# Two groups loaded two tokens to a partition, w spread by its DMA, and a new order of all steps

## The chip, the cores and the metric

The kernel runs on one core of a Trainium2 chip. The metric is device time in microseconds. The kernel before takes 174.13 us (median of three runs, 174.08 to 174.55).

A core has five engines that run side by side, each with an instruction queue of its own, worked off in order: TensorE (PE; PEld is its weight load), VectorE (DVE), ScalarE (ACT), GpSimd (POOL) and SyncE (SP), which here issues DMAs. An engine that waits for a semaphore holds up all that stands behind it in its queue.

## The reference

```python
def _attn_ref(r, k, v, w, u):            # B, H, S, D = 4, 8, 768, 48
    state = zeros((B, H, D, D))
    for t in range(S):
        cur = einsum('bhd,bhe->bhde', u * k_t, v_t)
        y[:, :, t] = einsum('bhd,bhde->bhe', r_t, state + cur)
        state = w * state + einsum('bhd,bhe->bhde', k_t, v_t)

def _moe_ref(x, w_in, w_out):            # 3072 tokens, 384, 2048
    h = x @ w_in
    g = where(h >= 1, h, where(h <= -1, 0, (h + 1) ** 2 / 4))
    return g @ w_out
```

The result of the first, token by token with its eight heads side by side, is the x of the second.

## The kernel before

The 768 tokens of a sequence are cut into six chunks of 128. A *unit* is one chunk of one batch, a *group* two batches of one chunk; there are 12 groups and 24 units, unit 2g + j being half j of group g. In a chunk the recurrence becomes matmuls: r is scaled by a rising power of w (`Rs`), k by a falling one (`Ks`), both are turned so that the head's dimension lies on partitions (into `TT`, or by a DMA into `RT`, `KT`), `A` is their product over all pairs of tokens, masked into `AT`; `Y` is `AT` times v, plus r times the state before the chunk; `Sp` is k times v, the chunk's addition to the state. The u term is the sum over d of r·k·u (`KU`, `RKU`, `us` into `diag`) times v (`B`), added to Y when y is written. y is turned (`X` and `xc`, or one DMA, `xcg`) into `xT`. Then the second part: `m` (12 matmuls) makes a quarter of h, `r`, `s`, `g` make the activation, `M` (4 matmuls) multiplies by a quarter of w_out, `og` copies the sum out of PSUM and `stg` stores it.

The order of all work is written out by hand in the string ORDER, which a loop reads from left to right. A word names a step, `do_` plus the letters: `Ks1.0=G/2` would be step Ks of group 1, half 0, on POOL (V is DVE, A is ACT), with PSUM bank 2. `m2.3` is quarter 3 of group 2, `M2.13` half 1, quarter 3. Each word puts instructions at the end of its engine's queue, so the string fixes the order in each queue and nothing else; semaphores do the rest. Loads (`LR`, `LK`, `LV`) go to SP's queue, as do the DMA transposes and the stores, while the weights (`WI`, `WO`) are issued on POOL. `Z` steps are idle matmuls on zeros that fill TensorE's gaps.

In groups 0 and 1 (JOINT = 2) the work goes unit by unit, with A, Y, Sp and X in eight PSUM banks b0 to b3 and pairs p0, p1; then b0 to b3 are closed (`first.close()`) and become the pairs p2, p3. The first `m` with /2 or /3 is `m1.1`, so it waits until every step in a bank is done. For the tables of powers, w is loaded as one row, its logarithm is spread over the partitions with a matmul (`bw`, L207), and ACT takes Exp with the token's number as the scale (`Wdn`, `Wup`; `dn_t`, `up_t` are copies that live in PSUM).

In the load below a packet holds one token of one head, 48 f32 numbers, 192 bytes:

```python
nc.sync.dma_start(out=t[:, j0 * H : j1 * H, :], in_=source(x, g, j0, j1))   # L253
```

Of the kernel before, what the change touches and what calls it, by code (L numbers as in the profile page):

```python
# [610 lines left out]
```

## Time and profile before

| | us |
|---|---|
| median of the runs | 174.13 |
| span of the profiled execution | 172.6 |
| TensorE busy | 164.4 |
| DVE, ACT, POOL busy | 130.6, 129.9, 117.4 |
| first `m` starts | 19.21 |
| last matmul ends | 169.14 |
| w_row to Ln, first table on ACT | 2.87, 5.12 |

The span counts from the first instruction to the last; the profiled execution's own time is not given beside it, so its distance to the runs is read from their median. The tables of the profile that matter here are the busy shares, the chain of work that ended last, the table of stretches (busy time of each engine, granted clock), the timeline of instructions, the groups of instructions with their mean duration, and the DMA issues with the time to landing. In a row such as `out<-in` the names are the program's; in a timeline row the first number is the start, the second the duration, and the bracket at the end the idle time before it and what ended it.

### The profile page before, as it was taken

What the parts mean: (1) busy time and instruction counts of PE and PEld (TensorE: products, weight loads), DVE (VectorE), ACT (ScalarE), POOL (GpSimd) and SP (SyncE); (2) the same over time, 40 slices, a digit from 0 to 9 for tenths busy, and PEclk for the clock granted to TensorE, in tenths of its full rate; (3) what the DMA queues carried; (4) which work ended last, traced back from release to release, by engine and by line L of the source; (5) the groups of instructions that cost most, each with busy time, mean ns of one, the idle gap of its engine ahead of it and who ended that gap; (6) DMA issues with size and microseconds to landing.
All of it is one profiled execution on the core that took longest, in us unless ns stands there. A gap on an engine that the chain in (4) does not pass through costs nothing.

```text
span 172.6 us, 4051 instructions
## 1 busy us (share of the span) xinstructions
PE 164.4 (95%) x1674; PEld 132.9 (77%) x1674; DVE 130.6 (76%) x150; ACT 129.9 (75%) x150; POOL 117.4 (68%) x86
## 2 busy tenths in 40 slices
PE   7989968999999999989999999999999999999991
PEld 5769868966889777588787797696897787888871
DVE  4578698988687688859789779885889959873752
ACT  4355698991699899189979879689695896988940
POOL 3496744998689949999999998999568804300000
PEclk9999999999999999999999999999999999999999
DMA  6999999998996999999999997998999025140022
GB/s 114 194 184 179 199 187 180 228 210 174 206 191 99 206 184 168 194 199 145 196 312 210 182 220 163 223 182 155 297 170 267 4 52 145 37 104 0 8 91 91
DMA packets 103751, 28.26 MB, mean 164 GB/s; under 512 B 98866, under 2 KB 102836, under 8 KB 103732
## 3 DMA queue, kind: packets, MB, share of 16 engines
q1 hardware_dynamic: 101824, 24.75, 79.9%
q0 software_dynamic: 1760, 3.15, 9.8%
q8 instruction: 13, 0.21, 0.6%
q10 hardware_dynamic: 148, 0.10, 0.2%
q14 instruction: 6, 0.05, 0.1%
HBM read 20.45 MB, written 4.72 MB: 146 GB/s over the span
## 4 chain that ended last, share of the span: by engine, by line
PE 87%; ACT 4%; DMA 2%; DVE 2%; issue 1%; POOL 0%; ACTq 0%; DVEq 0%
PE hp L475 35%; PE op L512 34%; PE A L370 4%; PE Y L438 3%; DMA xT<-y 2%; PE Y L432 2%; PE Sp L405 2%; PE z L566 2%; ACT pt L486 1%; PE T L330 1%; ACT TT L112 1%; PE lwp L207 1%; PE wp L233 1%; PE TR L330 1%; PE TK L330 1%
## 5 line engine op out<-in xcount | busy, mean ns | idle before, releaser
L475 PE MATMUL hp<-xT,w_in 128*128 128x256 bf16 x576 | 69.1, 273 | 1.3 <-DMA xT<-y 0.8
L512 PE MATMUL op<-w_out,g 128*128 128x384 bf16 (+1 forms) x400 | 68.4, 320 | 0.0
L498 DVE SCALAR_TENSOR_TENSOR g<-sq,hp 128x1024 bf16<-128x1024 bf16 x48 | 57.9, 1215 | 13.2 <-ACT sq L495 13.2
L475 PEld LDWEIGHTS <-w_in 128*128 128x128 bf16 x576 | 61.9, 114 | 4.6 <-issue 1.6
L486 ACT ACTIVATE pt<-hp 128x1024 f32<-128x1024 f32 x46 | 46.9, 1021 | 13.7 <-PE hp L475 13.7
L512 PEld LDWEIGHTS <-g 128*128 128x128 bf16 x400 | 37.5, 98 | 20.4
L495 ACT ACTIVATE sq<-pt 128x1024 bf16<-128x1024 f32 x46 | 48.3, 1057 | 1.2
L379 DVE TENSOR_TENSOR AT<-A,umask 128x1024 bf16<-128x1024 f32 x20 | 23.7, 1220 | 5.2 <-PE A L370 5.2
L282 POOL TENSOR_TENSOR Ks<-Ki,Wdn 128x768 bf16<-128x768 f32 (+1 forms) x12 | 20.3, 1689 | 8.5 <-ACT Wdn L225 3.4
L313 POOL TENSOR_TENSOR V<-Vb,diag 128x768 f32<-128x768 bf16 (+1 forms) x14 | 18.1, 1291 | 9.8 <-DVE diag L304 4.4
L282 POOL TENSOR_TENSOR RKU<-Ri,KU 128x768 f32<-128x768 f32 (+1 forms) x13 | 21.2, 1630 | 1.1 <-DVE KU L282 0.7
L282 POOL TENSOR_TENSOR KU<-Ki,u_sb 128x768 f32<-128x768 f32 (+1 forms) x13 | 21.2, 1634 | 0.4 <-DMA Ki<-in_k_dram 0.4
L416 POOL TENSOR_TENSOR state<-Tm,wCm 128x768 f32<-128x768 f32 x8 | 14.6, 1824 | 9.8 <-DVE Tm L413 9.8
L282 POOL TENSOR_TENSOR Rs<-Ri,Wup 128x768 bf16<-128x768 f32 x10 | 18.2, 1820 | 0.3 <-DMA Ri<-in_r_dram 0.3
L112 ACT CAST Vb<-Vi 128x768 bf16<-128x768 f32 (+1 forms) x14 | 10.2, 733 | 5.4 <-DMA Vi<-in_v_dram 5.4
L450 DVE TENSOR_TENSOR y<-Y,V 128x768 bf16<-128x768 f32 x10 | 9.6, 956 | 5.9 <-PE Y L438 3.3
L304 DVE TENSOR_REDUCE diag<-RKU 128x16 f32<-128x768 f32 (+1 forms) x14 | 11.6, 831 | 1.5 <-POOL RKU L282 1.5
L112 ACT CAST state_bf<-state 128x768 bf16<-128x768 f32 (+1 forms) x12 | 8.5, 717 | 4.4 <-POOL state L416 4.4
L112 ACT COPY o<-op 128x768 f32<-128x768 f32 (+1 forms) x9 | 6.7, 748 | 6.0 <-PE op L512 5.9
L438 PE MATMUL Y<-Vb,AT 128*128 128x48 bf16 x192 | 10.4, 186 | 0.4 <-ACT Vb L112 0.4
L438 PEld LDWEIGHTS <-AT 128*128 128x128 bf16 x192 | 9.5, 98 | 0.7 <-issue 0.5
L413 DVE TENSOR_TENSOR Tm<-Sp,state 128x768 f32<-128x768 f32 x8 | 7.7, 956 | 3.1 <-PE Sp L405 3.1
(73 smaller groups left out, 123.3 us busy)
## 6 DMA issues: line engine op xcount, KB each, us to landing
out_dram<-o SPq DMA_DIRECT2D x11, 384.0 KB, 3.8
Ki<-in_k_dram SPq DMA_DIRECT2D x9, 384.0 KB, 6.2
Ri<-in_r_dram SPq DMA_DIRECT2D x9, 384.0 KB, 6.2
Vi<-in_v_dram SPq DMA_DIRECT2D x9, 384.0 KB, 5.4
Ki<-in_k_dram SPq DMA_DIRECT2D x6, 192.0 KB, 4.0
Ri<-in_r_dram SPq DMA_DIRECT2D x6, 192.0 KB, 4.7
Vi<-in_v_dram SPq DMA_DIRECT2D x6, 192.0 KB, 6.0
w_in<-in_moe_w_in_dram POOLq DMA_DIRECT2D x2, 384.0 KB, 7.5
```

The source lines that it names most:

```text
L112: nc.scalar.copy(out, in_) if e == "A" else engines[e].tensor_copy(out, in_)
L282: engines[e].tensor_mul(part(out)[:, :, :, :D], part(a), rep(b, j1 - j0) if len(b.shape) == 3 and b.shape[1] == H else part(b))
L304: nc.vector.tensor_reduce(d[:, hs], tiles["RKU", g][:, hs, :], AX.X, ALU.add)
L313: engines[e].tensor_mul(t[:, hs, :], tiles["V", g][:, hs, :], tiles["diag", g][:, hs].unsqueeze(2).to_broadcast([P, n, D]))
L379: nc.vector.tensor_mul(t.rearrange("p i n t -> p (i n) t"), tiles["A", n].rearrange("p i (n t) -> p (i n) t", t=P), umask.unsqueeze(1).to_ ...
L416: engines[e].tensor_mul(states[g % BP], tiles["Tm", g], flat(wCm).unsqueeze(1).to_broadcast([P, UNITS, DM]))
L438: nc.tensor.matmul(Y[:, h * D : (h + 1) * D], AT[:, i, p, :], V[:, j * H + h, :], start=(c == 0), stop=True, skip_group_check=True,)
L475: nc.tensor.matmul(hp[:, f, :], w_in_sb[wi][:, i, wo * FG * P + f : (wo + 1) * FG * P : FG], tiles["xT", g][:, :, i, :], start=(i == 0), s ...
L486: nc.scalar.activation(t, tiles["hp", g, q], AF.Relu, bias=0.5, scale=0.5)
L495: nc.scalar.activation(t, p, AF.Square)
L498: nc.vector.scalar_tensor_tensor(out=make("g", ("g", g, q), [P, FG, TOK], BF16), in0=tiles["sq", g, q], scalar=1.0, in1=tiles["hp", g, q], ...
L512: nc.tensor.matmul(tiles[key][:, i, : o1 - o0], tiles["g", g, q][:, f, j * P : (j + 1) * P], w_out_sb[wi][:, wo, f * DO + o0 : f * DO + o1 ...
```

## The change

**Loads.** For groups 0 and 1, R and K come in one DMA each (no `.0`, `.1`). Partition 2q + b holds tokens 2q and 2q + 1 of batch b, so a packet has two tokens, 384 bytes. V is loaded as before.

**Parity.** Step `Rs0.1` now means the odd tokens of both batches, not batch 1; the same for `Ks` (into a tile `Kt`), `KU`, `RKU`, `us` and the transposes `TR`, `TK`. The copies out of PSUM, `cR` and `cK`, sort the columns back into units and so read with a stride. As the scaled k no longer lies token by token, `BK` turns it back on TensorE and `kc` copies it to SBUF, four units each. The u sums are also by parity; `dP`, four f32 matmuls per group with a selection matrix, sorts them, and `dC` copies them out.

**w.** Its DMA spreads it over 128 partitions; Ln and all Exp work on that, with tables `U0`, `U1`, `D0`, `D1` for the parities and `Wup`, `Wdn` for the other groups. `bw` and `wq` go; the column w_col comes by two DMAs of single elements, issued on ACT.

**Order.** All of ORDER is new. In the count, `r` on DVE goes from 2 to 9 (ACT 46 to 39), one each of `Rs`, `KU`, `B` and two of `Ks` of the later groups go from POOL to DVE, `og` on DVE from 3 to 1. `M` steps of one PSUM sum need no longer begin with quarter 0. The last group's two half outputs get a pair each, and both half stores are issued on SP (`stA11.1` was on ACT).

DVE's queue in the head. Before, from the copy of u on: the scaled K and R by unit, then masks and sums.

```order
L112 COPY u_sb_115<-up_153 128x384
L282 TENSOR_TENSOR Ks_92<-Ki_151,dn_t_174 128x8x48 x2
L282 TENSOR_TENSOR Rs_88<-Ri_158,up_t_183 128x8x48
L282 TENSOR_TENSOR KU_195<-Ki_151,u_sb_115 128x384
L282 TENSOR_TENSOR Rs_88<-Ri_158,up_t_183 128x8x48
L304 TENSOR_REDUCE diag_228<-RKU_198 128x8
L384 TENSOR_TENSOR AT_238<-A1_213,umask_105 128x512
L282 TENSOR_TENSOR Rs_89<-Ri_171,Wup_113 128x8x48 x2
L384 TENSOR_TENSOR AT_261<-A0_244,umask_105 128x512
```

The same place now, behind the scaled `Rs0.1`, `Ks0.0`, `Ks0.1` and two `KU` (`pt` are the parity tables, `TT` the sorted transposes, `pairs` the u sums by parity, `dP` their sorted form in PSUM):

```order
L115 COPY TT_233<-TK_212 128x512
L115 COPY TT_233<-TR_190 128x512
L115 COPY TT_228<-TK_212 128x512
L323 TENSOR_TENSOR Ks_104<-Ki_195,pt_197 128x8x48
L348 TENSOR_REDUCE pairs_270<-RKU_220 128x8
L337 TENSOR_TENSOR RKU_220<-Ri_174,KU_218 128x384
L456 TENSOR_TENSOR AT_274<-A1_252,umask_117 128x512
L456 TENSOR_TENSOR AT_274<-A0_251,umask_117 128x512
L348 TENSOR_REDUCE pairs_270<-RKU_220 128x8
L456 TENSOR_TENSOR AT_302<-A0_286,umask_117 128x512
L456 TENSOR_TENSOR AT_302<-A1_287,umask_117 128x512
L115 COPY diag_321<-dP_304 128x16
```

Three copies that ACT had made stand on DVE ahead of the first mask, and the copy of the sorted sums stands between the masks and what writes y.

SP's queue, where the program begins. Before, unit by unit:

```order
L253 DMA Ki<-in_k_dram 128x8x48 x2
L253 DMA Ri<-in_r_dram 128x8x48
L253 DMA Ki<-in_k_dram 128x8x48
L253 DMA Ri<-in_r_dram 128x8x48
L253 DMA Vi<-in_v_dram 128x8x48
L253 DMA Ri<-in_r_dram 128x8x48 x2
L253 DMA Ki<-in_k_dram 128x8x48
L253 DMA Vi<-in_v_dram 128x8x48 x3
```

Now, with the joint loads as 8 runs of 96 numbers:

```order
L274 DMA Ri<-in_r_dram 128x8x96
L274 DMA Ki<-in_k_dram 128x8x96 x2
L281 DMA Vi<-in_v_dram 128x8x48 x2
L274 DMA Ri<-in_r_dram 128x8x96
L281 DMA Vi<-in_v_dram 128x8x48 x2
L281 DMA Ki<-in_k_dram 128x8x48 x2
```

R of group 0 now comes first, and two units of V stand ahead of R of group 1.

DVE's queue around the sum of y in group 7. Before:

```order
L379 TENSOR_TENSOR AT_1682<-A_1660,umask_105 128x1024
L379 TENSOR_TENSOR AT_1701<-A_1651,umask_105 128x1024
L498 SCALAR_TENSOR_TENSOR g_1703<-sq_1643,hp_1628 128x1024
L450 TENSOR_TENSOR y_1730<-Y_1705,V2_1649 128x768
L498 SCALAR_TENSOR_TENSOR g_1766<-sq_1738,hp_1684 128x1024
```

Now:

```order
L451 TENSOR_TENSOR AT_1712<-A_1690,umask_117 128x1024
L451 TENSOR_TENSOR AT_1722<-A_1699,umask_117 128x1024
L570 SCALAR_TENSOR_TENSOR g_1754<-sq_1679,hp_1660 128x1024
L485 TENSOR_TENSOR Tm_1760<-Sp_1737,state_147 128x768
L522 TENSOR_TENSOR y_1794<-Y_1764,V2_1789 128x768
L570 SCALAR_TENSOR_TENSOR g_1809<-sq_1792,hp_1724 128x1024
```

The state's sum `Tm` has moved ahead of the sum of y. On TensorE the words between the last Y of this group and its first `m` are, before and now:

```
Y14/0 Y15 ... m6.3/1 m6.2/2 ... Sp12/0 Sp13 ... M6.00/3 M6.10 M6.11 M6.01 ... m7.1/0
Y15/3 Y14 ... m6.2/2 ... m6.3/1 ... M6.01/3 M6.11 M6.00 ... m7.1/0
```

The core of the diff:

```diff
-    nc.scalar.dma_start(out=w_row, in_=w.rearrange("(o h) d -> o (h d)", o=1))
+    nc.scalar.dma_start(out=w_all, in_=w.rearrange("(o h) d -> o (h d)", o=1).to_broadcast([P, DM]))
...
+    nc.gpsimd.memset(w_col, 1.0)
+    for j in range(2):
+        nc.scalar.dma_start(out=w_col[j * HP : j * HP + D, :], in_=w.rearrange("(p j) d -> j d p", j=2)[j])
...
     def do_ln(e, b):
-        nc.scalar.activation(lnw[:, :, :D], w_row.rearrange("o (h d) -> o h d", h=H), AF.Ln)
+        nc.scalar.activation(w_all, w_all, AF.Ln)
...
+    def do_U(e, b, i):
+        nc.scalar.activation(paired("up2")[:, i], w_all, AF.Exp, scale=up2_col[i])
...
     def load(x, what, cls, g, j):
+        if g < JOINT and what != "V32":
+            t = make(cls, (what, g), [P, UNITS * H, D], F32)
+            b0 = g * UNITS
+            nc.sync.dma_start(
+                out=t.rearrange("p (h e) d -> p h (e d)", e=2),
+                in_=x[b0 : b0 + UNITS, :, :C, :].rearrange("b h (q e) d -> q (b h) (e d)", e=2),
+            )
+            return
...
+    def do_dP(e, b, g):
+        t = tiles["dP", g] = bank(b[0], [P, UNITS, H], F32, "dP")
+        for j in range(UNITS):
+            for i in range(2):
+                nc.tensor.matmul(t[:, j], sel[j][:, 1 + j - i : 1 + j - i + P], tiles["pairs", g][:, i * H : (i + 1) * H], start=(i == 0), stop=(i == 1))
...
+    def unpair(e, kind, n, i):
+        g, j = divmod(n, UNITS)
+        t = make("TT", ("TT", n), [P, 2 * NP, P], BF16)[:, i * NP : (i + 1) * NP]
+        copy(e, t.rearrange("x p (q e) -> x p q e", e=2), tiles[kind, g].rearrange("x e p (q b) -> x p q e b", b=2)[..., j])
...
+    def do_BK(e, b, n):
+        t = tiles["BK", n] = bank(b[0], [P, NP, P], BF16, "BK")
+        for p in range(NP):
+            nc.tensor.transpose(t[:, p, :], tiles["TT", n][:, NP + p, :], ident)
+
+    def do_kc(e, b, n):
+        g, j = divmod(n, UNITS)
+        copy(e, flat(scaled("Ks", g)[:, j * H : (j + 1) * H, :]), tiles["BK", n].rearrange("p n t -> p (n t)"))
```

217 lines of the change are left out of this document (126 added, 91 removed).

## The prediction

> **What bounds the kernel now.** First the page's busy shares, then the chain of work that ended last in order of time, then the table of stretches and the waits.
>
> ```profile
> PE 164.4 (95%) x1674; PEld 132.9 (77%) x1674; DVE 130.6 (76%) x150; ACT 129.9 (75%) x150; POOL 117.4 (68%) x86
> ...
> 19.28 1.45 PE hp L475 x12
> ...
> 27.27 6.73 PE hp L475 x60
> ...
> 57.76 1.31 PE hp L475 x12
> 59.07 0.65 PE op L512 x4
> ...
> 64.63 0.55 PE A L370 x16
> ...
> 69.80 4.27 DMA xT<-y
> 74.11 1.47 PE hp L475 x12
> ...
> 89.83 2.63 PE hp L475 x24
> ...
> 169.14 0.33 ACT o L112
> 169.49 0.36 DVE o L112
> ```
>
> ```profile
> 20.00:24.00 4.00, 3.03 (x42) 2.55 (x41) 3.70 (x8) 3.23 (x4) 1.24 (x2) 1.00 1.14 208
> 24.00:28.00 4.00, 3.12 (x41) 2.89 (x40) 3.68 (x7) 2.83 (x5) 1.92 (x3) 1.00 0.88 163
> ...
> 68.00:75.00 7.00, 6.16 (x73) 4.16 (x69) 6.01 (x6) 3.09 (x4) 6.92 (x5) 1.00 1.01 192
> ```
>
> The columns of the stretches are length, busy time of PE, PEld, DVE, ACT, POOL, then granted clock, DMA share, GB/s. TensorE is the bound: the chain lies on it from 19.28 us, the first `m0.0`, to 169.14, and its clock is full. One `m` step (12 matmuls) takes 1.31 us, one `M` (4) 0.65, one `AA` (16) 0.55. TensorE can win only what it idles, in three places. **The head** runs until `m1.1`, 27.27 + 1.31 = 28.58 us; by then both kernels have done the same: A, Y, X, Sp of four units and the four `m` of group 0. From 20 to 28 us TensorE idles 0.97 + 0.88 us, and before 19 us its gaps are filled with idle matmuls (`Z`). **The dense part**, 28.58 to 169.14, is 140.56 us and holds one gap of 0.84 us in 68 to 75. **The tail** is what follows 169.14. The span is 172.6 us and the runs' median 174.13, so 1.5 us lies around the span; I take that as unchanged.
>
> **The change, part by part.**
>
> *Tables.* In place of `bw`, four Exp and eight small matmuls there are a spread load of w, two element loads, Ln on all partitions and four Exp.
>
> ```profile
> 0.74 0.54 ACTq L127 DMA_DIRECT2D w_row<-in_w_dram  x1
> 1.31 0.23 ACTq L128 DMA_DIRECT2D u_row<-in_u_dram  x1
> 2.87 0.52 ACT L203 ACTIVATE lnw<-w_row 1x384 f32<-1x384 f32 x1
> 5.12 0.58 ACT L225 ACTIVATE Wdn<-lwp,dn_col 128x384 f32<-128x384 f32 x1 [1.73 <-PE lwp L207]
> 5.60 0.55 ACT L219 ACTIVATE dn_t<-lwp,dn_col 128x384 f32<-128x384 f32 x1
> Ki<-in_k_dram SPq DMA_DIRECT2D x1, 192.0 KB, 3.0
> 4.00:8.00 4.00, 4.00 (x15) 2.81 (x14) 1.60 (x4) 1.50 (x3) 1.81 (x2) 1.00 1.40 195
> ```
>
> The spread w is 192 KB. It lands between 2.87 (where Ln could start before) and 0.74 + 3.0 = 3.7 (the first load of K, equally large). Two more issues on ACT, 0.23 to 0.54 us each, stand ahead of Ln: it starts at 3.3 to 4.2, I take 3.7. Ln takes 0.55 and its reader waits for its end; each Exp follows the last by 0.48. So `U1` ends at 4.8, `U0` 5.3, `D0` 5.8, `D1` 6.2. Before, the first table ended at 5.70 and the second at 6.15.
>
> *Loads.* At 195 GB/s 192 KB pass in 1.0 us, so the first load spent 3.0 - 1.0 = 2.0 us on its way. A joint load of 384 KB costs 2.0 us at that rate. The other end comes from stores, whose packets are larger:
>
> ```profile
> out_dram<-o SPq DMA_DIRECT2D x1, 192.0 KB, 1.9
> out_dram<-o SPq DMA_DIRECT2D x1, 96.0 KB, 1.7
> ```
>
> 96 KB more cost 0.2 us, so 384 KB 0.8. 384 bytes are nearer to 192 than to a store's row: I take 1.4. With 0.3 for w, R of group 0 lands at 0.74 + 2.0 + 0.3 + 1.4 = 4.4, K at 5.9, K of group 1 at 7.3, two units of V by 9.2, R of group 1 at 10.6. By the Trainium skill, "DMA: Bandwidth & Descriptors", section Specifications, transfers under 512 B stay below line rate; no row here has 384-byte packets. By that the joint load stands at its dear end, which is rival B.
>
> *DVE sets the head.* From `Rs0.1` on it has 24 instructions in a row that lead to the last `xc` before `m0.0`.
>
> ```profile
> 11.34 1.02 DVE L282 TENSOR_TENSOR Rs<-Ri,Wup 128x384 bf16<-128x384 f32 x2
> L384 DVE TENSOR_TENSOR AT<-A,umask 128x512 bf16<-128x512 f32 x8 | 5.2, 685 | 0.9 <-PE A L370 0.9
> L112 DVE COPY TT<-TR 128x512 bf16<-128x512 bf16 x1 | 0.4, 414 | 0.0
> L233 PE MATMUL wp<-ones,lnw 1*128 1x1 f32 x8 | 1.7, 329 | 0.0
> L282 POOL TENSOR_TENSOR RKU<-Ri,KU 128x384 f32<-128x384 f32 x3 | 3.0, 1002 | 0.8 <-DVE KU L282 0.7
> 10.79 2.48 POOL L244 DMA_DIRECT2D w_in<-in_moe_w_in_dram  x3
> 10.08 0.61 PE L370 MATMUL A<-TT 48*128 48x128 bf16 x8
> L112 ACT CAST Vb<-Vi 128x384 bf16<-128x384 f32 x4 | 1.9, 508 | 1.3 <-DMA Vi<-in_v_dram 1.3
> L313 POOL TENSOR_TENSOR V<-Vb,diag 128x384 f32<-128x384 bf16 x4 | 3.3, 828 | 5.0 <-DVE AT L384 2.0 <-ACT Vb L112 1.4 <-ACT w_col L236 1.1
> ```
>
> Two 384-wide products take 1.02 us, one 0.55. A 512-wide mask takes 0.69, a copy of 512 from PSUM 0.41; the new `cK`, `cR` read it with a stride, so 0.41 (same operation) to 0.69 (as many elements, one by one): I take 0.60. The Trainium skill, "VectorE: DVE Perf Modes", section "Mode 2×_1P", lets two bf16 values be packed only at a step of ±1; the 0.41 agrees with packing, and by the rule the strided copy would cost 0.69, which on three copies is 0.3 us later, 173.7.
>
> Then: `Rs0.1` at 4.9; `Ks0.0` at 6.0 (K lands 5.9); `KU0.1` ends 7.95; three strided copies to 9.45, so `A1` starts at 9.5 (the first A before: 10.07). `Ks1.1`, `us0.0`, `RKU0.1`, two masks, `us0.1` end at 12.55. Now comes what was not there: `dP0` is four f32 matmuls that pass as eight, and eight such took 1.7 us. `dP0` 12.6 to 14.3, with DVE's two masks beside it and then 1 us of idle DVE; `dC0` to 14.5. `Rs1.0`, `B0.1`, `KU1.1`, `y1`, `y0`, `xc1`, `kc2`, `xc0` follow to 17.8. ACT's `cR3` ends at 17.6, so `A3` and then `m0.0` at **18.0**, 1.2 us earlier than 19.2.
>
> Behind it the same again: POOL runs `RKU1.1`, `KU1.0`, `RKU1.0` from 16.0 to 19.0, `us1.0` ends 20.0, `dP1` 20.05 to 21.75 stands ahead of `m0.1` on TensorE. ACT's `dC1` and the cast of V wait for it (22.4), POOL's two `B1` end at 24.1, DVE's state, `y2`, `y3` at 25.85, `g0.1` (1.2) at 27.0, two states and two `xc` at 28.55. `m1.1` starts at **28.6**, against 28.58: 0.0. The four back-transposes (`BK`, four matmuls and so 0.3 us each by the row of eight in 0.61), `kc` on ACT and the idle matmuls lie in TensorE's gaps. The ends: Ln at 3.3, copies at 0.41 and loads at 0.8 give K at 4.7, `Ks0.0` at 5.4 and three copies cheaper by 0.5, -1.1; copies at 0.69 and loads at 2.0 (K at 7.0) give 1.1 + 0.3, +1.4.
>
> *The weights* w_in are issued at 8.6 (behind `RKU0.0`), 2.2 us earlier than 10.79, and w_out's last half, used first, at 24.2; none was waited for before, and I count nothing.
>
> *Dense part.* The matmuls are the same ones. What can wait is a group's first `m`, on the DMA transpose of y:
>
> ```profile
> 52.63 0.96 DVE L450 TENSOR_TENSOR y<-Y,V 128x768 bf16<-128x768 f32 x1 [1.01 <-PE Y L438]
> 53.62 1.31 SPq L467 DMA_TRANSPOSE xT<-y  x1
> DMA to landing us min/median/max: 2.7/3.0/4.3
> 90.44 0.95 DVE L450 TENSOR_TENSOR y<-Y,V 128x768 bf16<-128x768 f32 x1
> L486 ACT ACTIVATE pt<-hp 128x1024 f32<-128x1024 f32 x46 | 46.9, 1021 | 13.7 <-PE hp L475 13.7
> L483 DVE TENSOR_SCALAR pt<-hp 128x1024 f32<-128x1024 f32 x2 | 2.4, 1220 | 0.0
> ```
>
> From the last Y (52.53 in group 3, 53.62 - 0.96 - 0.13) to xT it is 0.1 + 0.96 + 0.03 + 3.0 = 4.1 us, and 4.6 where DVE came 0.6 late (Y ended at 89.83, y began at 90.44). Matmuls put between them were 4.45 us in group 4, where the transpose took 4.3 and TensorE lost 0.84. They are now 4.57 in groups 3, 6, 7, 11, 4.79 in group 4, 4.9 in group 10 and more elsewhere. Group 4 should lose at most 0.5, the others nothing up to 0.2: together I take -0.5, ends -0.84 and +1.0. `r` moves from ACT (1.02) to DVE (1.22) seven times more; DVE goes from 130.6 to about 142 us of 172.6, POOL down by some 8; both still have room.
>
> *Tail.* The two half outputs now have PSUM pairs of their own, so `oB11.1` no longer follows `oA11.1` (0.36), but both half stores are issued on SP, and two group stores come late ahead of them: -0.2, ends -0.36 and +0.4.
>
> **Sum:** 0.0 - 0.5 - 0.2 = -0.7 us on the span; 174.13 - 0.7 = **173.4**.
>
> **The rivals.**
> - *B, the loads gain nothing per byte.* K of group 0 lands at 0.74 + 2.0 + 0.3 + 4.0 = 7.0 and `Ks0.0`, with everything behind it on DVE, is 1.1 us later: 174.5. For it: 384 is near 192. Against: the store rows.
> - *C, slower: the sum of y comes one DVE operation late.* In group 7 the order puts `g` and `Tm` between the mask and y; if one `g` (1.215) still runs when Y ends, the way to xT is 5.3 against 4.57 us of cover. That is 0.7 in each of groups 3, 6, 7, 11: +2.9, 176.3. It decides from a delay of 0.5 us; the rows show 0.6 once (90.44) and 0.1 at 52.63.
> - *D, faster: the f32 pass is cheap.* If a `dP` costs what eight bf16 matmuls do (0.61), `dC0` comes 1.1 earlier, and the second one shortens `m0.1` and `dC1`: `m1.1` at 27.1, 171.9. For it: the 8 wp matmuls may have waited on issue. Against: they did follow each other at 0.2 us.
> - *E, nothing:* the dense part gives back 0.7 in small new waits: 174.1.
>
> **How the numbers follow.** Chances: forecast 0.44, B 0.14, C 0.13, D 0.17, E 0.12. About 0.3% (0.5 us) is what a measurement of this kernel can tell from no change. Faster: most of the forecast (0.37) and D, 0.54. Same: 0.07 of the forecast, most of B and E, 0.26. Slower: C and the rest, 0.20. Range: the head's cheap end and the dense part's give 173.4 - 1.1 - 0.34 = 172.0; the dear ends of head and dense part together would be 176.3, and as they need not meet I stop at 175.6. That leaves out C and the lower half of D, about 2 in 10.
>
> **What would show it.** `m0.0` near 18.0 and `m1.1` near 28.6; eight matmuls of a `dP` near 1.7 us; `Ks0.0` at 6.0; strided copies at 0.6; no wait for xT over 0.5. It is wrong if `m1.1` starts over 1 us away from 28.6, if TensorE waits for xT in several groups, or if w_out's halves come after their first use.

## The result and the profile after

| | before | after |
|---|---|---|
| median of four runs each, us | 174.11 (174.04 to 174.55) | 180.10 (179.77 to 180.63) |
| span of the profiled execution | 172.6 | 178.9 |
| first `m` starts | 19.21 | 22.74 |
| head: five `m` steps, `m0.2` to `m1.2`, end | 34.00 | 37.79 |
| last matmul ends | 169.10 | 175.49 |
| rest: from the head's end to the last matmul | 135.10 | 137.70 |

The changed kernel is **slower**: the ratio is 1.034, 95% interval 1.032 to 1.036. The forecast was 173.4. Its profiled execution took 180.63, so 1.7 us lie around the span. In the experiments below one run each of e10, e12 and e14 fell into a slower state of the core (181.93, 183.25 and 183.78 us) and is left out of their medians.

The two marks are read from the timeline. In both kernels the five `m` steps from `m0.2` on run as one block of 60 matmuls, and at its end all `m` of groups 0 and 1 are done; before, this is the row of 27.27 + 6.73 quoted above. After, with the block of matmuls that ends last (169.14 above is the start of the copy behind it, the matmuls end at 169.10):

```profile
30.97 6.82 PE L547 MATMUL hp<-xT,w_in 128*128 128x256 bf16 x60
...
168.79 6.70 PE L584 MATMUL op<-w_out,g 128*128 128x384 bf16 x56
```

So the head lost 3.8 us, the rest 2.6, and the tail gained 0.1 (178.9 - 175.49 = 3.4 against 3.5). In the expectations below "m1.1 ends at 28.58 (32.44)" stands for where `m1.1` starts; only the differences are used.

The page of the changed kernel, busy shares and the chain by engine:

```profile
PE 167.0 (93%) x1694; PEld 133.9 (75%) x1694; DVE 148.7 (83%) x176; ACT 126.5 (71%) x148; POOL 109.1 (61%) x83
...
PE 63%; DMA 12%; DVE 12%; POOL 6%; issue 3%; SPq 1%; ACT 0%; DVEq 0%; POOLq 0%
```

DVE has 18.1 us more than before, though the moved work was to cost it some 11. The table of stretches, columns as before:

```profile
12.00:16.00 4.00, 2.37 (x26) 1.80 (x27) 4.00 (x5) 1.79 (x5) 3.38 (x4) 1.00 1.29 203
16.00:20.00 4.00, 3.98 (x39) 3.72 (x34) 3.66 (x8) 0.85 (x2) 1.00 (x1) 1.00 1.20 202
20.00:24.00 4.00, 4.00 (x45) 3.13 (x43) 3.87 (x10) 2.48 (x5) 3.35 (x4) 1.00 1.13 208
...
68.00:75.00 7.00, 7.00 (x84) 5.52 (x83) 6.72 (x8) 6.28 (x8) 6.95 (x5) 1.00 1.25 202
```

From 12 to 16 us DVE is busy throughout with five instructions while TensorE has 2.37 of 4 us of work: DVE sets the head, as forecast, but with instructions that take far too long. The timeline of the changed kernel's head:

```profile
5.58 0.52 ACT L230 ACTIVATE w_all<-w_all 128x384 f32<-128x384 f32 x1 [2.58 <-DMA w_all<-in_w_dram]
...
8.17 1.04 DVE L323 TENSOR_TENSOR Ks<-Ki,pt 128x384 bf16<-128x384 f32 x2 [0.37 <-DMA Ki<-in_k_dram]
...
11.28 0.68 DVE L115 COPY TT<-TK 128x512 bf16<-128x512 bf16 x1
...
12.70 1.01 POOL L323 TENSOR_TENSOR Ks<-Ki,pt 128x384 bf16<-128x384 f32 x1
12.94 2.14 DVE L337 TENSOR_TENSOR RKU<-Ri,KU 128x384 f32<-128x384 f32 x1
...
13.66 1.00 POOL L317 TENSOR_TENSOR Rs<-Ri,pt 128x384 bf16<-128x384 f32 x1
...
16.34 1.05 PE L354 MATMUL dP<-pairs,sel 128*128 128x8 f32 x4
...
18.10 1.01 PE L390 MATMUL TK<-ident,Ks 128*128 128x128 bf16 x8
18.28 0.17 DVE L115 COPY diag<-dP 128x16 f32<-128x16 f32 x1 [0.34 <-PE dP L354]
...
18.61 1.00 POOL L366 TENSOR_TENSOR V<-Vb,diag 128x384 f32<-128x384 bf16 x1 [3.21 <-DVE diag L115]
18.84 1.18 DVE L366 TENSOR_TENSOR V<-Vb,diag 128x384 f32<-128x384 bf16 x1
```

Two things stand out. Ln starts at 5.58 instead of the forecast 3.7, and `Ks0.0` at 8.17 instead of 6.0. And `RKU0.1`, one product of 0.55 us before, takes 2.14: POOL's `Ks1.0` and `Rs1.1` run from 12.70 to 14.66, and DVE's product ends 0.42 after the second. `B0.1` at 18.84 likewise ends 0.41 after POOL's `B0.0`.

In the rest TensorE has these gaps of over 0.4 us (before: one, 0.84); each costs some 0.16 more than its bracket shows, since a row's duration runs into the gap (twelve matmuls of `m` are given as 1.47 and follow each other in 1.31):

```profile
42.55 0.38 PE L383 MATMUL T<-ident,Rs 128*128 128x128 bf16 x4 [0.41 <-DVE g L570]
50.01 0.20 PE L504 MATMUL Y<-state_bf,TT 128*128 128x96 bf16 x1 [0.54 <-DVE AT L451]
99.78 1.47 PE L547 MATMUL hp<-xT,w_in 128*128 128x256 bf16 x12 [0.57 <-DMA xT<-y]
...
132.68 1.58 PE L547 MATMUL hp<-xT,w_in 128*128 128x256 bf16 x13 [0.74 <-DVE Tm L485]
```

The first two stand behind `Rs2` and `Ks3`, which DVE took from POOL: 1.73 and 1.99 us there, against 0.95 for the same kind of product (`KU9`) beside an idle POOL.

### The profile page after: what moved, and what is told of

Read it like the earlier page. It is cut to its first block, busy times and chain, and to the rows that moved or that the text cites. A ratio compares the mean times of both kernels' runs of the same rounds, so it can differ in the third digit from the quotient of the medians.

```text
span 178.9 us, 4094 instructions
## 1 busy us (share of the span) xinstructions
PE 167.0 (93%) x1694; PEld 133.9 (75%) x1694; DVE 148.7 (83%) x176; ACT 126.5 (71%) x148; POOL 109.1 (61%) x83
## 4 chain that ended last, share of the span: by engine, by line
PE 63%; DMA 12%; DVE 12%; POOL 6%; issue 3%; SPq 1%; ACT 0%; DVEq 0%; POOLq 0%
PE hp L547 28%; PE op L584 23%; DMA xT<-y 4%; DMA Ki<-in_k_dram 4%; PE A L442 3%; DMA Ri<-in_r_dram 3%; PE Y L510 2%; POOL Rs L313 2%; DVE g L570 2%; DMA RT<-Rs 2%; DVE y L522 2%; PE dP L354 2%; PE Y L504 1%; PE Sp L477 1%; DVE AT L451 1%
## 5 line engine op out<-in xcount | busy, mean ns | idle before, releaser
L584 PEld LDWEIGHTS <-g 128*128 128x128 bf16 x400 | 37.4, 98 | 20.4 <-DVE g L570 0.2
L558 ACT ACTIVATE pt<-hp 128x1024 f32<-128x1024 f32 x39 | 39.8, 1021 | 14.5 <-PE hp L547 13.4
L567 ACT ACTIVATE sq<-pt 128x1024 bf16<-128x1024 f32 x39 | 41.2, 1058 | 1.1
L366 POOL TENSOR_TENSOR V<-Vb,diag 128x768 f32<-128x768 bf16 (+1 forms) x12 | 16.3, 1358 | 22.8 <-DVE diag L348 10.8
L313 POOL TENSOR_TENSOR Rs<-Ri,Wup 128x768 bf16<-128x768 f32 x9 | 16.5, 1829 | 6.2 <-DMA Ri<-in_r_dram 6.1
L313 POOL TENSOR_TENSOR RKU<-Ri,KU 128x768 f32<-128x768 f32 x10 | 18.2, 1824 | 1.6 <-DMA Ri<-in_r_dram 1.3
L313 POOL TENSOR_TENSOR KU<-Ki,u_sb 128x768 f32<-128x768 f32 x9 | 16.4, 1823 | 0.3 <-DMA Ki<-in_k_dram 0.3
L313 POOL TENSOR_TENSOR Ks<-Ki,Wdn 128x768 bf16<-128x768 f32 x8 | 14.6, 1828 | 2.2 <-DMA Ki<-in_k_dram 2.2
L115 ACT COPY o<-op 128x768 f32<-128x768 f32 (+1 forms) x11 | 8.3, 757 | 7.1 <-PE op L584 7.1
L565 ACT ACTIVATE sq<-pt 128x1024 bf16<-128x1024 f32 x9 | 9.5, 1056 | 5.0 <-DVE pt L555 4.9
L555 DVE TENSOR_SCALAR pt<-hp 128x1024 f32<-128x1024 f32 x9 | 11.0, 1220 | 0.8 <-PE hp L547 0.8
L348 DVE TENSOR_REDUCE diag<-RKU 128x16 f32<-128x768 f32 x10 | 9.4, 945 | 2.2 <-POOL RKU L313 2.2
L510 PE MATMUL Y<-Vb,AT 128*128 128x48 bf16 x192 | 10.6, 186 | 0.1
```

Of the source, the lines that this page charges most:

```text
L115: nc.scalar.copy(out, in_) if e == "A" else engines[e].tensor_copy(out, in_)
L313: engines[e].tensor_mul(part(out)[:, :, :, :D], part(a), rep(b, j1 - j0) if len(b.shape) == 3 and b.shape[1] == H else part(b))
L366: engines[e].tensor_mul(t[:, hs, :], tiles["V", g][:, hs, :], tiles["diag", g][:, hs].unsqueeze(2).to_broadcast([P, n, D]))
L510: nc.tensor.matmul(Y[:, h * D : (h + 1) * D], AT[:, i, p, :], V[:, j * H + h, :], start=(c == 0), stop=True, skip_group_check=True,)
L558: nc.scalar.activation(t, tiles["hp", g, q], AF.Relu, bias=0.5, scale=0.5)
L567: nc.scalar.activation(t, p, AF.Square)
```

## The experiments

Theories. **T1**: the spread load of w and its extra issues delay the tables and the first loads. **T2**: DVE's products of two SBUF tiles are held up by POOL. **T3**: the parity's own steps, above all `dP`, are on the path. **T4**: the new order of the rest costs 2.6 us by itself. Medians are of four runs (e11: twelve; e10, e12 and e14: three), in five sets, each beside the kernel before (174.1 to 174.3); marks are those of one profiled execution.

| run | median | head ends | rest |
|---|---|---|---|
| changed kernel | 180.10 | 37.79 | 137.70 |
| e1 new head, old rest | 181.03 | 38.25 | 137.40 |
| e2 old head, new rest | 180.89 | 33.81 | 141.78 |
| e3 w as one row | 179.11 | 36.55 | 137.40 |
| e4 five products on POOL | 180.24 | 37.71 | 138.90 |
| e5 `RKU0.1` ahead | 178.48 | 35.98 | 137.80 |
| e6 no `dP` | 181.01 | 38.78 | 137.11 |
| e7 e2 with w_out early | 176.36 | 34.20 | 138.74 |
| e8 e4, `Rs2` on DVE | 180.06 | 37.72 | 137.26 |
| e9, e13 e3 + e5 + two moves | 180.44, 180.17 | 36.03, 36.54 | 138.03, 138.58 |
| e10 192-byte packets | 179.76 | 37.90 | 138.00 |
| e11 before, patched | 174.38 | 33.98 | 135.22 |
| e12 idle matmuls for `dP` | 179.63 | 37.44 | 138.37 |
| e14 e13, gaps filled | 180.44 | 35.86 | 139.43 |
| e15 changed, gaps filled | 180.76 | 38.57 | 139.07 |
| e16 two waits of the rest | 179.84 | 37.64 | 136.14 |
| e17 head put right | 177.67 | 35.49 | 136.83 |
| e18 e17 + e16 | 178.92 | 35.70 | 137.30 |

How far can a mark be trusted? e1, e4, e8 and e16 have the order of the changed kernel's head, and their heads end between 37.64 and 38.25 (the changed kernel's at 37.79). e9 and e13 are one kernel and differ by 0.5 us in either mark. So a difference of marks below some 0.6 us says little. Nor is the profiled execution always near the median: in e4, e7 and e15 it was the slowest of the four (181.76, 177.98 and 182.78), in e9 and e16 the fastest (179.24 and 178.94).

**e1, e2, e7: the halves apart.** ORDER is cut ahead of `m1.1`; e1 has the changed kernel to there and the old words behind, e2 the reverse, e7 issues the half of w_out that the new rest uses first in the old head.

```diff
 # e7 against e2, in the old head
-WO0 WO1
+WO2
```

> The head of the changed kernel (loads, parity, w, its order up to the first m1.1) with the order of before from m1.1 on. In the profiles the new head ends m1.1 at 32.44 us, the old one at 28.58, and from there to the last matmul the changed kernel takes 143.09 us, the one before 140.56. If the two losses are independent (theory), the first m1.1 ends near 32.4, the rest takes 140.6 and the time is 174.1 + 3.9 = 178.0. Rival: the rest was slow only because the head left it late buffers and transfers; then this kernel's rest is slow too, and the time is near 180.

> The head of the kernel before with the new order from m1.1 on. Theory (independent losses): m1.1 ends near 28.6, the rest takes 143.1, the time is 174.1 + 2.5 = 176.6. Rival (the rest suffers from the new head): the rest takes about 140.6 and the time is 174.1 to 174.5.

> As the run with the old head and the new rest, but w_out's last half, which the new rest uses first, is issued in the old head in place of the first two quarters (the run before waited 4.05 us for it). Theory: the new order's rest costs 2.5 us more than the old one's behind any head: m1.1 ends at 28.4, the rest takes 143.1, time 176.6. Rival: without that wait the new rest is as good as the old one behind a head that ends early, and only the new head is slow: 174.0 to 174.6.

The timeline of e1, then of e2:

```profile
79.64 1.47 PE L544 MATMUL hp<-xT,w_in 128*128 128x256 bf16 x12 [2.13 <-DMA xT<-y]
```

```profile
37.86 5.74 PE L514 MATMUL op<-w_out,g 128*128 128x384 bf16 x24 [4.05 <-DVE g L500]
```

e2's wait is an artefact of the cut: w_out's last half came behind the first two (the row names g, but in e7, with that half issued first, 0.55 of it is left, for w_out). Without it, e7 is 2.2 us slower than the kernel before (ratio 1.014, 1.008 to 1.020), near T4's 2.5; the 0.55 that is left of the cut is part of it. But e1 came out against T4, and near its rival: the *old* rest, 135.1 behind its own head, takes 137.4 behind the new one. Group 4's transposed y, for which TensorE waited 0.84 before, came 2.13 late. So the new rest is some 2 us dearer behind either head, and the old one loses as much when the new head stands before it.

**e3: T1.**

```diff
-    nc.scalar.dma_start(out=w_all, in_=w.rearrange("(o h) d -> o (h d)", o=1).to_broadcast([P, DM]))
+    nc.scalar.dma_start(out=w_row, in_=w.rearrange("(o h) d -> o (h d)", o=1))
...
-        nc.scalar.activation(w_all, w_all, AF.Ln)
+        nc.scalar.activation(w_row, w_row, AF.Ln)
...
+        nc.tensor.matmul(t, ones, w_row, start=True, stop=True)
...
-        nc.scalar.dma_start(out=w_col[j * HP : j * HP + D, :], in_=w.rearrange("(p j) d -> j d p", j=2)[j])
+            nc.sync.dma_start(out=w_col[j * HP : j * HP + D, :], in_=w.rearrange("(p j) d -> j d p", j=2)[j])
```

> The changed kernel, but w comes as one row, its logarithm is taken on one partition and spread by a matmul, as before; the column of single elements is issued on SP behind the first two loads of V instead of on ACT. Theory T1 (the spread of w and its two extra issues hold back the tables and, on the DMA engines, the first loads of R and K): Ln starts near 2.9 instead of 5.58, R0 and K0 land about 1 us earlier (5.6 and 7.0), Ks0.0 starts at 7.1 instead of 8.17, m1.1 ends 1.0 to 1.5 us earlier: time 178.6 to 179.1. Rival: R0 and K0 land as late as before because joint loads are slow by themselves, and the head's end does not move: 180.1, or slower where the element loads now hold back R1.

The DMA issues of the first 2 us, KB and us to landing, in the changed kernel and in e3:

```profile
Ri<-in_r_dram SPq DMA_DIRECT2D x1, 384.0 KB, 5.9
Ki<-in_k_dram SPq DMA_DIRECT2D x1, 384.0 KB, 6.5
w_all<-in_w_dram ACTq DMA_DIRECT2D x1, 192.0 KB, 4.4
```

```profile
Ri<-in_r_dram SPq DMA_DIRECT2D x1, 384.0 KB, 4.1
Ki<-in_k_dram SPq DMA_DIRECT2D x1, 384.0 KB, 4.8
```

R and K land 1.7 to 1.8 us earlier (K at 1.53 + 4.8 = 6.3 instead of 8.0): T1's load half is shown for the spread load and the element loads together, as e3 takes both out of the way of R and K. The head gained 1.24, the time 1.0. But the timeline says that most of it was not this:

```profile
7.43 1.47 DVE L329 TENSOR_TENSOR Ks<-Ki,pt 128x384 bf16<-128x384 f32 x2
...
12.62 1.20 DVE L343 TENSOR_TENSOR RKU<-Ri,KU 128x384 f32<-128x384 f32 x1
...
13.34 1.32 POOL L323 TENSOR_TENSOR Rs<-Ri,pt 128x384 bf16<-128x384 f32 x1
```

`Ks0.0` and `Ks0.1` start 0.74 earlier and take 0.43 longer, beside POOL's `Rs0.0`; then `RKU0.1` takes 1.20 instead of 2.14, as it came between POOL's two products, the second of which took 1.32 instead of 1.00. In both kernels it starts 0.24 us behind POOL's first product and 0.72 ahead of its second, so these rows do not show what decides whether DVE comes between.

**e5: T2 in the head.**

```diff
-... Ks1.1=V WI0 BK1/2 us0.0=V V0.0=A RKU0.1=V AT1.1=V
+... RKU0.1=V Ks1.1=V WI0 BK1/2 us0.0=V V0.0=A AT1.1=V
```

> The changed kernel with one word moved: RKU0.1 (R times KU, odd tokens of group 0, on DVE) stands ahead of Ks1.1 and us0.0 in DVE's queue, so that it runs while POOL does nothing. Theory T2 (DVE's product of two SBUF tiles is held until POOL's running product ends, and again by the one behind it: 2.14 us in the changed kernel, beside POOL's Ks1.0 and Rs1.1, against 0.55 before): it takes 0.55 us at about 11.9, the masks, the sum and dP0 come 1.2 to 1.6 us earlier, m1.1 ends at 30.9 to 31.3 instead of 32.44, time 178.5 to 179.0. Rival T1 (late tables and loads set the head): the time it frees turns into a wait for K and R of group 1, and m1.1 moves by less than 0.4.

```profile
11.65 0.68 DVE L337 TENSOR_TENSOR RKU<-Ri,KU 128x384 f32<-128x384 f32 x1
12.26 0.55 DVE L323 TENSOR_TENSOR Ks<-Ki,pt 128x384 bf16<-128x384 f32 x1
```

One word moved, nothing else: the head ends 1.8 us earlier and the time falls by 1.6 (ratio to before 1.025, 1.019 to 1.032). T2 is shown for this product, as expected. The size in the time is less sure than in the head: the four runs lie between 177.53 and 179.88, and the slowest is among those of the changed kernel.

**e6, e12: T3.** e6 leaves the selection matmuls out, e12 (below) puts 16 and 20 idle ones in their place.

```diff
-                nc.tensor.matmul(t[:, j], sel[j][:, 1 + j - i : 1 + j - i + P], tiles["pairs", g][:, i * H : (i + 1) * H], start=(i == 0), stop=(i == 1))
+        idling(bank(b[0], [P, P], F32, "z"), 16 if g == 0 else 20)
...
-tiles["dP", g])
+tiles["pairs", g].rearrange("p (j h) -> p j h", j=UNITS))
```

> The changed kernel without the selection matmuls dP0 and dP1: dC copies the u sums as they lie, by parity (it leaves out the sorting of the u sums into batches). Theory T3 (the parity's own extra steps are on the path): TensorE's transposes behind dP0 start 1.8 us earlier, dC0 does not wait (0.34), m0.1 and dC1 come 0.9 earlier, m1.1 ends 1.0 to 1.5 us earlier: 178.6 to 179.1. Rival T2 (DVE, full from 6.8 to 22.5 us, sets the head): at most the 0.34 of DVE's wait and what dP1 holds back, 0.4 together: 179.7.

> As the run without the selection matmuls, but idle matmuls stand in their place (it leaves out the sorting of the u sums). Without them m0.0's twelve matmuls took 2.5 us instead of 1.3, and the masked products beside it 0.61 instead of 0.40, and the time was 0.9 longer. Theory: TensorE's clock was still at half rate, as it had had less to do; with idle matmuls m0.0 takes 1.3 again at about 22.4, the five m steps end at 37.2 to 37.8 instead of 38.8, time 179.6 to 180.2. Rival: m0.0 was slow for another reason (weights or xT arriving in pieces): 181.0.

The first `m` of e6, then of e12:

```profile
22.47 2.75 PE L544 MATMUL hp<-xT,w_in 128*128 128x256 bf16 x12
```

```profile
22.18 1.50 PE L544 MATMUL hp<-xT,w_in 128*128 128x256 bf16 x12
```

T3 fell. Without `dP` the first `m` starts only 0.27 earlier, and its twelve matmuls take 2.75 us instead of 1.50, as at half speed. With idle matmuls in the place of `dP` they take 1.50 again: its matmuls, like the idle ones, had helped to keep TensorE's speed up. The head then ends 0.35 earlier than in the changed kernel, less than heads of one order differ by themselves, and of the three runs (179.61 to 180.97) one lies above all of the changed kernel's. So a cost of `dP` is not seen; the idle matmuls take TensorE's time too, so e12 does not price `dP` alone.

**e10: are larger packets quicker?**

```diff
-            nc.sync.dma_start(
-                out=t.rearrange("p (h e) d -> p h (e d)", e=2),
-                in_=x[b0 : b0 + UNITS, :, :C, :].rearrange("b h (q e) d -> q (b h) (e d)", e=2),
+            for e in (1, 0):
+                nc.sync.dma_start(
+                    out=t.rearrange("p (h e) d -> p e h d", e=2)[:, e],
+                    in_=x[b0 : b0 + UNITS, :, :C, :].rearrange("b h (q e) d -> e q (b h) d", e=2)[e],
```

> The changed kernel with each joint load of R and K split into two DMAs, one per parity (the odd tokens first), so that a packet has 192 bytes again; partitions and all else stay. In the changed kernel the joint loads landed 1.4 us apart. If 384-byte packets are what makes them quick (384 KB at the 195 GB/s of before would take 2.0), R and K of group 0 land 0.6 and 1.2 us later and Ks0.0 starts at 9 or later instead of 8.17: time 180.6 to 181.5. Rival (rival B of the prediction, nothing gained per byte): they land as before or earlier, as the halves come one by one, and the time is 179.8 to 180.2.

The stretch from 4 to 6 us in e10 and in the changed kernel (last column GB/s):

```profile
4.00:6.00 2.00, 1.73 (x8) 0.56 (x6) 0.00 (x0) 0.00 (x0) 0.00 (x0) 1.00 1.14 202
```

```profile
4.00:6.00 2.00, 2.00 (x8) 0.84 (x8) 0.00 (x0) 0.42 (x1) 0.00 (x0) 1.00 1.12 285
```

They are: 285 against 202 GB/s. (With 384-byte packets e3 moves 272 in the same stretch; with 192-byte ones the kernel before moves 201.) `Ks0.0` starts at 9.01 instead of 8.17, though not for that alone: Ln, too, came 1.2 us later, at 6.79. The time did not follow (179.76, where 180.6 to 181.5 was expected), as `RKU0.1` met POOL otherwise again (1.20 us).

**e4, e8, e16: the rest's waits.** e4 puts `Rs2`, `Ks3`, `B2`, `Ks6`, `KU9` back on POOL, e8 all but `Rs2`, e16 is e8 with `Tmg8` ahead of `us10`, which waits for POOL.

```diff
-Rs2=V  Ks3=V B2=V Ks6=V KU9=V   us10=V Tmg8=V
+Rs2=G (e4)  Ks3=G B2=G Ks6=G KU9=G (all)   Tmg8=V us10=V (e16)
```

> The changed kernel with five products of the later groups (Rs2, Ks3, B2, Ks6, KU9) back on POOL, at the same places of the order. Theory T2 (a DVE product that runs beside POOL's takes two to three times as long, 1.73, 1.91 and 1.9 us for Rs2, Ks3, Ks6 against 0.95 without, and holds up g, AT and T behind it): DVE's busy time falls by 7.4 us, the waits of TensorE at 42.5 and 50 us (0.41 and 0.54) go, and the time is 179.1 to 179.6. Rival: POOL, now with five more products of 1 to 2 us each, is late instead, and the time is 180.1 or more.

> As the run with five products back on POOL, but Rs2 stays on DVE, so that POOL is not late with the issue of w_out (there TensorE waited 0.81 us for w_out). Theory T2: the wait of TensorE for AT at 50 us (0.54, behind Ks3 with 1.91 us on DVE) goes and none takes its place: the rest takes 142.5 instead of 143.1, time 179.5. Rival: the five products were not what the rest waits for; the transfer of y in group 4 is late as in the run with five products (TensorE waited 2.2 us there, 0 in the changed kernel): 180 to 181.

> The changed kernel with two edits behind m1.1: Ks3, B2, Ks6 and KU9 on POOL, as in the run of that name, and Tmg8 ahead of us10 on DVE. There us10 waits 2.19 us for POOL's RKU10, Tmg8 stands behind it, and m8.2 waits for the PSUM pair that Tmg8 reads: a gap of 0.91 us from the last matmul ahead of it. Theory (the rest lost its 2.6 us in five such gaps): the gap goes, from the five m steps to the last matmul it takes 136.3 us instead of 137.7 (the old order: 135.1), time 179.0 to 179.3. Rival: the time comes back in a later wait, for the transposed y or for DVE: 179.8 or more.

Two waits of e4 in the place of the two that went:

```profile
41.12 1.46 PE L584 MATMUL op<-w_out,g 128*128 128x384 bf16 x8 [0.81 <-DMA w_out<-in_moe_w_out_dram]
80.53 2.78 PE L547 MATMUL hp<-xT,w_in 128*128 128x256 bf16 x24 [2.20 <-DMA xT<-y]
```

In e4 and e8 the wait at 50 us went, in e4 the one at 42.5 too. But POOL also issues w_out, in e4 now late, and the transfer of y took up to 5.9 us to land there (before at most 4.3), up to 4.6 in e8. e16's rest is 1.6 shorter in its trace, with no wait for `Tm`, as expected; its median gained 0.3, not the 0.8 to 1.1 expected. The profiled execution was the best of its four.

**e9, e13, e14, e15: the head's remaining 2 us.** e9 is e3 and e5 with `Rs1.0` and `KU1.1` ahead of `dC0`; e13 the same again; e14 fills TensorE's gaps in it, e15 those of the changed kernel.

```diff
-Z13/3 A1/01 ... Zp7/0 A0/31
+Z20/3 A1/01 ... Zp15/0 A0/31 ... Zp4/0 dP0/0    (e15: Zp18, no Zp4)
```

> The changed kernel with w as one row (as in the run of that name), RKU0.1 ahead of Ks1.1 (as in the run of that name), and Rs1.0 and KU1.1 ahead of dC0, where POOL does nothing. With w as one row alone the load of K let DVE start 0.74 us earlier, but 0.42 of that went into a product that waited for POOL. Theory: T1 and T2 are independent once DVE's products run beside an idle POOL: the five m steps from m0.2 to m1.2 end at 35.98 (RKU0.1 ahead alone) - 0.7 (w) - 0.4 (no product of DVE beside POOL's B0.0) = 34.9 us, against 37.8 in the changed kernel and 34.0 before; time 178.5 - 1.1 = 177.4. Rival: the head now waits for K and R of group 1 or for TensorE's slow clock, and gets no earlier than 35.6: 178.1 or more.

> The kernel of the run with w as one row and the moved products, once more, as the base of the next one (its four runs lay far apart). In its trace the five m steps ended at 36.03 us, no earlier than with RKU0.1 moved alone (35.98), though DVE now waits (0.51 us for Y); TensorE's granted clock was 0.50 from 14 to 21 us. Theory: the same head end, about 36.0, and 178.4. Rival: the head ends at 35 and the last trace was a disturbed one: 177.4.

> The same kernel with more idle matmuls ahead of A1 (20 instead of 13), ahead of A0 (15 instead of 7) and four ahead of dP0, which fill TensorE's gaps from 10.9 to 14.4 us. Theory (TensorE's slow clock holds the head: from 14.4 to 21 us it has no gap, but every transposition takes 1.0 us for 8 instead of 0.6): the clock stays at 1.0, dP0 takes 1.2 instead of 1.9, the two TK and two TR 0.6 instead of 1.03 each pair, m0.0 starts at 19.6 to 20.2 instead of 21.0, the five m steps end 0.8 to 1.4 earlier than in the run before: 177.0 to 177.6. Rival: the clock drops all the same, as the selection matmuls and Y are too little work for it, and nothing moves (178.4) or the idle matmuls delay A0 (178.8).

> The changed kernel, with nothing else, with 20 idle matmuls instead of 13 ahead of A1 and 18 instead of 7 ahead of A0. Theory: there DVE, full from 6.8 to 22.5 us, sets the head, and a faster TensorE takes away only DVE's wait for dP0 (0.34) and up to 0.4 before m0.0: 179.4 to 179.9. Rival: the slow clock alone is what made the new head late: the five m steps end at 36.5 instead of 37.8, 178.8.

e9, table of stretches (the column behind POOL is the granted clock), then e15's first `m`:

```profile
14.00:16.00 2.00, 1.78 (x15) 1.61 (x10) 2.00 (x5) 1.02 (x3) 1.27 (x2) 0.54 1.12 188
16.00:18.00 2.00, 2.00 (x24) 1.84 (x25) 1.79 (x6) 0.78 (x2) 0.82 (x1) 0.50 1.19 188
```

```profile
22.38 2.67 PE L547 MATMUL hp<-xT,w_in 128*128 128x256 bf16 x12
```

e9 and e13 gained nothing over e5 in the head, and their medians are 1.7 to 2.0 us above e5's, which stays unexplained. In the head the earlier start went into `Ks0.0` beside POOL's `Rs0.0` (1.46 for two instead of 1.03), and the two moved products put `dC0` 0.4 later. Filling the gaps kept TensorE fast through `dP0` and the transposes behind it (eight in 0.61 us, at 15.56 in e14 and 17.29 in e15). Then it waited 0.92 us for `dC0` and the clock fell (e14); in e15 it fell about 18 us and was still down in the first `m` (2.67). Neither run is faster than its base, but neither kept the clock up to the head's end. So what a full clock would be worth there is not shown.

**e17, e18: the causes together.**

```diff
-Z17/0 bu/1 ln=A LR0 U1=A LK0 Rs0.1=V U0=A uS=V ... Rs0.0=G Ks0.0=V ... Ks0.1=V
+Z17/0 ln=A bw/1 bu/3 LR0 U1=A LK0 Rs0.1=V U0=A Rs0.0=V ... Ks0.0=V ... Ks0.1=V uS=V
 # and w as in e3, RKU0.1 as in e5; e18: and the edits of e16
```

> The changed kernel with w as one row (its spreading matmul ahead of u's), RKU0.1 ahead of Ks1.1, and Rs0.0 on DVE instead of POOL, with the copy of u behind Ks0.1, so that none of DVE's first products runs beside POOL. In the run with w as one row R and K of group 0 landed 1.7 us earlier than in the changed kernel, but the tables stood behind u's matmul and Ks0.0 waited for POOL's Rs0.0. Theory (late tables and loads, and products beside POOL, are all that made the new head late): the first table ends at 5.7, DVE is through KU0.1 at 9.3 instead of 9.94 in the run with RKU0.1 moved alone, dP0 starts at 13.9, m0.0 at 20.2 and the five m steps end at 35.3 instead of 35.98 there; time 177.9. Rival: TensorE's slow clock takes it back: the five m steps end at 36 or later, 178.5 or more.

> The same with the two edits behind m1.1 (Ks3, B2, Ks6, KU9 on POOL, Tmg8 ahead of us10). Theory: the parts add up; the stretch from the five m steps to the last matmul is 1.2 us shorter than in the run before, time 176.7 to 177.0, and the changed kernel with all of it taken out is still not faster than the one before (174.1), as the transposed y of groups 4 and 6 still comes late. Rival: head and rest together lose nothing to a late y: 175.5 or less.

e17's timeline, DVE's products now beside an idle POOL, and the head's end:

```profile
5.68 1.03 DVE L323 TENSOR_TENSOR Rs<-Ri,pt 128x384 bf16<-128x384 f32 x2 [2.06 <-ACT pt L249]
...
6.63 1.02 DVE L329 TENSOR_TENSOR Ks<-Ki,pt 128x384 bf16<-128x384 f32 x2
...
28.67 6.82 PE L553 MATMUL hp<-xT,w_in 128*128 128x256 bf16 x60
```

`KU0.1` ends at 9.2 (expected 9.3), `dP0` starts at 13.8 (13.9), the head ends at 35.49 (35.3), the time is 177.67 (177.9). e18 fell: with two waits of the rest taken away it is 1.2 us *slower* than e17 (178.13 to 179.59 against 177.32 to 178.17), and its rest is no shorter (137.30 against 136.83). The waits of the rest do not add up; in these traces others come in their place.

**e11: the kernel before, patched.**

```diff
-xcg4 m4.0/1 ... AT10 ... Sp8/2 Sp9        M11.10/0 M11.11 ... (one pair for both halves)
+xcg4 AT10 Sp8/2 Sp9 m4.0/1               MA11.10/0 MA11.11 ... MB11.10/1 MB11.11
```

> The kernel before with two edits that the traces point to: Sp8 and Sp9 stand ahead of m4.0, where TensorE waits 0.84 us for the transposed y (0.33 us of matmuls move into the wait), and the last group's two half outputs have PSUM pairs of their own, so that the second copy does not wait for the first (0.36). Theory: both lie on the path: 174.1 - 0.33 - 0.36 = 173.4 to 173.6. Rival: the transfer of y or the last store sets the end anyway: 174.0 to 174.2.

Ratio 0.999 (0.996 to 1.002): no difference. `Sp8` and `Sp9` moved into the wait, and the transposed y then came 0.2 us later (`m4.0` at 74.34 instead of 74.11); the last store is issued at 169.63 instead of 169.87. No version found beats the kernel before.

## Why the prediction was wrong

**Tables (predicted: Ln at 3.3 to 4.2).** It started at 5.58. Two steps failed. The first is "It lands between 2.87 ... and 3.7 (the first load of K, equally large)": 192 KB spread from one row took 4.4 us to land, not 3.0, so until 5.1. The second is "Two more issues on ACT, 0.23 to 0.54 us each": they are that short, but the second, which stands ahead of Ln, began only at 5.15. In e10 w had landed at 0.73 + 3.5 = 4.2, and Ln still came right behind that issue. The changed kernel, then e10:

```profile
5.15 0.39 ACTq L188 DMA_DIRECT2D w_col<-in_w_dram  x1
```

```profile
6.43 0.32 ACTq L188 DMA_DIRECT2D w_col<-in_w_dram  x1
6.79 0.52 ACT L230 ACTIVATE w_all<-w_all 128x384 f32<-128x384 f32 x1 [3.79 <-DMA w_col<-in_w_dram]
```

What held the issue back is not shown; e3 and e17 take the spread and both issues off ACT's way at once.

**Loads (predicted: 1.4 us per joint load, R at 4.4, K at 5.9).** The size was right: R landed at 0.74 + 5.9 = 6.6, K at 1.54 + 6.5 = 8.0, so 1.4 apart, and without the spread load K came at 6.3. Rival B did not happen. But they landed 2.2 and 2.1 us later than forecast, of which 1.8 and 1.7 go with the spread load and the element loads (e3).

**DVE in the head (predicted: `RKU0.1` 0.55).** This is the largest miss: 2.14, and 1.6 us of the time by e5. The durations came from rows of before in which POOL happened to be idle: there `RKU0.1` ran from 13.93 to 14.48, and POOL's next product began at 14.36. The new order put POOL's products beside DVE's, and I priced each by its own row and never laid the two queues side by side. The Trainium skill, "SBUF — State Buffer", section "Who interferes with whom", says that a DVE instruction with two SBUF inputs contends with a GpSimd instruction that reads SBUF, and that the order of issue decides who is held up. The rows agree that DVE's product ends behind POOL's (by 0.42 and 0.41 us). But by the order of the starts `RKU0.1` (12.94) should have come behind `Ks1.0` and ahead of `Rs1.1` (13.66), at 13.71 + 0.42 = 14.13, so in 1.2 us, as in e3 and e10; in the changed kernel it waited for both.

The prediction also put a moved table at nothing. In the kernel before, the tables that DVE read while POOL worked lay in PSUM (`dn_t`, `up_t`), and there two products took 1.01 us although POOL worked from 7.18 to 8.18:

```profile
6.88 1.01 DVE L282 TENSOR_TENSOR Ks<-Ki,dn_t 128x384 bf16<-128x384 f32 x2
7.18 1.00 POOL L282 TENSOR_TENSOR KU<-Ki,u_sb 128x384 f32<-128x384 f32 x1 [0.40 <-DMA Ki<-in_k_dram]
```

The changed kernel has its tables in SBUF (`pt`), and the same pair took 1.47 beside POOL in e3. No run puts them back into PSUM.

**Strided copies (predicted 0.60, ends 0.41 and 0.69).** 0.68. The rule of the Trainium skill, "VectorE: DVE Perf Modes", cited in the prediction, was right, the choice between the ends was not; three copies, 0.24 us.

**`dP` (predicted 1.7, on the path, twice).** The eight passes took 1.9 and 1.1, so rival D's 0.61 was wrong too. What they cost on the path is not resolved (e12: 0.35, within the spread of the marks). `m0.0` to the start of `m1.1` took 9.5 us, not 10.6; 0.6 of the difference is the second `dP`.

**Head (predicted 0.0).** +3.8. By e5, 1.8 is DVE waiting for POOL in one instruction; with the late tables and loads and POOL's `Rs0.0` put right too, 2.3 (e17). The other 1.5 stays open. In e17's trace `B0.1` still takes 1.18 beside POOL's `B0.0`, and TensorE is at half speed again from `dP0` (13.8) to 20.4 us, but no run separated these; e14 and e15, which went for the clock, did not shorten the time and did not keep the clock up.

**Dense part (predicted -0.5).** +2.6. "DVE goes from 130.6 to about 142 ... both still have room" is the step that failed: 148.7, and TensorE waited for DVE three times. The cover in front of the transposed y was enough in group 4 (no wait; before 0.84) and short in group 6, where y began as soon as Y was done (94.72) and the transfer took 4.0 us instead of 3.0. Rival C, y one DVE operation late in groups 3, 6, 7 and 11, did not happen; the slower side came by other ways. No single wait makes up the 2.6 us: e4, e8, e16 and e18 took waits away, and no median fell by more than 0.3. By e1 and e7 it hangs on head and rest together; which of the meetings between transfers and queues decide it stays open.

**Tail (predicted -0.2).** -0.1.

## What to carry to other kernels

A duration from a row holds only for what ran beside it: before an operation with two SBUF operands moves to DVE, or DVE's queue is shifted, lay POOL's timeline beside DVE's and price the overlap as the rest of what POOL has running, and see whether one operand lies in PSUM, as here before. A load that feeds the first table is not priced by its bytes alone, nor the issues that stand ahead of its reader by their own length, above all when the loads that everything waits for are issued with it. An order fitted by hand belongs to one timing: a better order of one half has to be judged with the other half as it will then run.

## What the runs showed of the hardware

TensorE's granted clock stands at 1.00 in the changed kernel's head, and yet eight transposes take 1.01 us at 18.10 and eight matmuls of `A` 0.61 at 12.01, against 0.40 at 22.41. In e9, which records 0.50 from 14 to 21 us, eight transposes take the same 1.01. So the record can stand at 1.00 while TensorE is slow; here durations tell more. The Trainium skill, "TensorE: Matmul & The Clock Gate", Part 1, has the slow clock as the default that sustained work lifts; the rows agree: in the kernel before, with 60 idle matmuls ahead of the first `m` instead of 43, four transposes go from 0.58 at 15.14 to 0.39 at 17.33, in the changed kernel full speed comes at 22.4. Being busy is not all that counts: in e9 TensorE is busy for 6.78 of the 7 us from 14 to 21, with f32 matmuls of eight columns, bf16 ones of 48 and transposes among them, and the record stands at 0.50 to 0.54 throughout.

DVE's product waited through two POOL products in a row in eight kernels (2.14 or 2.15 us), and in two came between them (1.20 in e3 and e10, where POOL's second took 1.32 and 1.33), at the same distance of the three starts: 0.9 us that these rows do not let one foresee.
